# Attention and hash-routed experts on one core: loads four pairs ahead, casts three ahead, scatters queued behind the casts, the table filled in four pieces

## The chip, the cores and the metric

The kernel runs on one core of a Trainium2 chip. The metric is the device time of one execution in microseconds (us). Engines are named as in the profile: PE (TensorE) with its weight loads PEld, DVE (VectorE), ACT (ScalarE), POOL (GpSimd), SP (SyncE). A "q" behind a name is the engine's sequencer, which issues DMAs.

## The reference

Self-attention over 8 batches, 8 heads, 576 positions of 64 values in float32, with a relative position bias from a table of 32 buckets, is followed by a hash-routed mixture of 8 experts:

```
scores = q @ k^T / sqrt(64) + bias_table[bucket(|i - j|)]
x      = softmax(scores) @ v                 # 4608 tokens x 512
e      = token_id * 2654435761 % 8           # expert of a token
out    = relu(x @ w1[e]) @ w2[e]             # w1: 512 x 1024, w2: 1024 x 512
```

## The kernel before

**Attention** runs over 32 pairs of heads (4 pairs a batch). `load` (L165) brings q, k and v of a pair as float32 by eight DMAs on SP's queue, into tiles with four buffers (`qf`, `kf`, `vf`). `cast_qk` and `cast_v` (L187, L197) make float16 of them on POOL. `transposes` (L378) turns q and k on PE into PSUM (`pq`, `pk`, from the tag `aux` with two buffers, which `px` shares) and copies them on DVE to `qt` and `kz`. `scores` (L414) makes five score tiles in a two-buffer PSUM tile `ps`; ACT takes the exponential (L436, and L464 for the short fifth tile `atts`, of which there is one a pair), and DVE multiplies the band near the diagonal by `ebd` (L452, L469), the exponential of the bias. `av_steps` (L473) multiplies by v on PE into `px`, and DVE normalises into `x_all` (L501, L502). The scores of pair n are interleaved on PE with the products of pair n-1. All 45 product matmuls, 18 score matmuls and 12 transposes of a pair are placed by hand in PE's program; the order on the other engines is made by the scheduler of the framework.

In iteration n the program loads, casts and transposes pair n+2. After the last pair of a batch `dispatch` (L515) issues five indirect DMAs on POOL, which scatter the batch's tokens to the rows of their expert in the table `t_xperm`. The table is first filled with a padding row `zx` by one DMA of 5140 KB on ACT's queue (`fill_table`, L275). `route` (L281) computes each token's row from the token ids; it is called in iteration 1. The bias becomes `ebd` by two small matmuls (L234), an exponential (L239), one DMA to the DRAM tensor `t_f` (L243) and 16 DMAs back (L254), half on SP's queue and half on ACT's. The weights of the first two experts are loaded with a cast to float16 by POOL's queue (`load_w1`, `load_w2`; in program order at iteration 20 and behind the last, but the scheduler moved them to the start).

**A DMA's semaphore.** The framework gives the DMAs of SP and ACT together eight semaphores in turn (POOL's have eight of their own). A DMA waits at its issue until the one eight places earlier in that turn has landed.

**Experts**: per expert, a table block of 640 rows is loaded (`x_load`, L572), turned (L588), multiplied by w1 (L607), put through ReLU on ACT (L613), multiplied by w2 (L625), copied (L632) and scattered to the output (L633). This part is the same in both kernels but for the order of the first block loads.

Of the kernel before, what the change touches and what calls it, by code (L numbers as in the profile page):

```python
# [11 lines left out]
F32 = mybir.dt.float32  # L12
# [19 lines left out]
def kernel(  # L32
# [71 lines left out]
    F_d = nc.dram_tensor("t5_f", [H, D // 2, FW + 1], F16, kind="Internal")  # L104
# [41 lines left out]
    with tc.tile_pool(name="at", bufs=1) as at, tc.tile_pool(  # L146
# [40 lines left out]
        def cast_qk(n):  # L187
            for dst, src, name in ((qh, qf, "qh"), (kh, kf, "kh")):
                dst[n] = at.tile([PB, 2 * NBLK, 2, D], F16, name=name, bufs=3)
                nc.gpsimd.tensor_copy(  # L190
                    out=dst[n][:, :, :, :].transpose([0, 2, 1, 3]),
                    in_=src[n][:, :, :, :].rearrange(
                        "p h k (c d) -> p h (k c) d", c=2
                    ),
                )
# [8 lines left out]

        for n in range(2):
            load(n)

        tbl = at.tile([NB, H], F32, name="tbl")
        nc.sync.dma_start(out=tbl[:, :], in_=bias_table)
        ohsb = at.tile([NB, FW], F32, name="ohsb")  # L210
        nc.scalar.dma_start(out=ohsb[:, :], in_=OH_d.ap())
        nc.sync.dma_start(out=ident[:, :], in_=I128_d.ap())

        cast_qk(0)
        cast_qk(1)
        for i, z in enumerate(kz):
            nc.vector.memset(z[D:P, :, 0, :], 0.0)
            nc.vector.memset(z[:D, :, 1, :], 0.0)
        for i, x in enumerate(va):
            for hh in range(2):  # L220
                r0, r1 = D * hh, D * hh + D
                o0, o1 = D - D * hh, P - D * hh
                c0 = hh * (D + 1)
                nc.gpsimd.memset(x[o0:o1, :, c0 : c0 + D + 1], 0.0)
                nc.gpsimd.memset(x[r0:r1, :, c0 + D : c0 + D + 1], 1.0)
            if i < 2:
                cast_v(i)

        bps = atp.tile([P, 3, 512], F32, name="bps", tag="ps", bufs=2,
                       space=bass.MemoryType.PSUM)  # L230
        FH = (FW + 1) // 2
        for i in range(2):
            f0, f1 = FH * i, min(FH * i + FH, FW)
            nc.tensor.matmul(  # L234
                out=bps[:H, i, : f1 - f0], lhsT=tbl[:, :],
                rhs=ohsb[:, f0:f1],
            )
        ebsb = at.tile([H, 2, FH], F16, name="ebsb")
        nc.scalar.activation(  # L239
            out=ebsb[:, :, :], in_=bps[:H, :2, :FH], func=AF.Exp, bias=0.0,  # L240
            scale=1.0,
        )
        nc.sync.dma_start(  # L243
            out=F_d.ap()[:, :, :FW],
            in_=ebsb[:, :, :].rearrange("h a b -> h (a b)")[:, :FW]
            .unsqueeze(1).to_broadcast([H, HD, FW]),
        )
        for o in range(2):
            for c in range(2):
                for hh in range(2):  # L250
                    for cj in range(2):
                        eng = nc.sync if hh == 0 else nc.scalar
                        r0 = D * hh + HD * cj
                        eng.dma_start(  # L254
                            out=ebd[r0 : r0 + HD, :, c, o, :],
                            in_=bass.AP(
                                F_d.ap().tensor,
                                hh * HD * (FW + 1) + (o - cj + 1) * FY
                                + MAXD - 1 - D - HD * c,
                                [[FW, HD], [2 * HD * (FW + 1), NPAIR],  # L260
                                 [1, WB]],
                            ),
                        )
        nc.sync.dma_start(out=tok[:, :], in_=TOK_d.ap())
        nc.sync.dma_start(out=msk[:, :], in_=MSK_d.ap())
        nc.sync.dma_start(out=sltsb[:, :], in_=SLT_d.ap())
        tid32 = moe_token_ids.bitcast(I32)
        nc.sync.dma_start(
            out=er[:, :], in_=bass.AP(tid32.tensor, 0, [[2 * S, B], [1, 2 * S]])
        )  # L270
        zx = at.tile([P, XW], F16, name="zx")
        nc.gpsimd.memset(zx[:, :DM], 0.0)
        nc.gpsimd.memset(zx[:, DM:XW].bitcast(I32), BIG)

        def fill_table():  # L275
            nc.scalar.dma_start(
                out=xperm_d.ap()[:NSLOT, :].rearrange("(p r) d -> p r d", p=P),
                in_=zx[:, :].unsqueeze(1).to_broadcast([P, NSLOT // P, XW]),
            )
# [98 lines left out]
        def transposes(n):  # L378
            b, m = pairs[n]
            pq = aux([P, S], F16, "pq")  # L380
            pk = aux([P, S], F16, "pk")
            for k3 in range(NBLK):
                for c in range(2):
                    x = 2 * k3 + c
                    o = UA * c + PB * k3 if k3 < 2 else QW + UB * c
                    nc.tensor.transpose(  # L386
                        out=pq[:, o : o + PB],
                        in_=qh[n][:, x, :, :].rearrange("p h d -> p (h d)"),
                        identity=ident[:PB, :PB],
                    )  # L390
            for k3 in range(NBLK):
                for c in range(2):
                    x = 2 * k3 + c
                    o = HALF * c + PB * k3
                    nc.tensor.transpose(
                        out=pk[:, o : o + PB],
                        in_=kh[n][:, x, :, :].rearrange("p h d -> p (h d)"),
# [3 lines left out]
            nc.vector.tensor_copy(out=qt[:, :], in_=pq[:, :])  # L401
            z = kz[n % 3]
# [9 lines left out]
            qts[n], ktz[n] = qt, z  # L412

        def scores(n, g):  # L414
# [10 lines left out]
            if g < NDUO:  # L425
# [13 lines left out]
                )  # L439
                u0 = max(D * g - D, 0)  # L440
# [15 lines left out]
            else:  # L456
                kt = z[:, 2 * NDUO, :, :].rearrange("p h u -> p (h u)")
                for r in range(2):
                    nc.tensor.matmul(
                        out=ps[:, r, :HALF], lhsT=kt,  # L460
                        rhs=qt[:, HALF * r : HALF * r + HALF],
                        start=True, stop=True,
                    )
                nc.scalar.activation(  # L464
                    out=ats[:, :].rearrange("p (r i) -> p r i", r=2),
                    in_=ps[:, :2, :HALF], func=AF.Exp, bias=0.0, scale=scale,
                )
# [5 lines left out]
        def av_steps(n):  # L473
# [3 lines left out]
            for its in ((0, 1, 2), (3, 4)):  # L477
# [34 lines left out]
                )  # L512
                yield

        def dispatch(b):  # L515
            for t in range(NIT):
                sc_in = nc.gpsimd.indirect_dma_start(  # L517
                    out=xperm_d.ap()[:, :],
                    out_offset=bass.IndirectOffsetOnAxis(
                        ap=ds2[:, B * t + b : B * t + b + 1], axis=0  # L520
# [256 lines left out]
```

## Time and profile before

| | us |
|---|---|
| median of 3 runs (544.93 to 824.42) | 544.97 |
| the profiled execution's own time | 544.6 |
| its span, first to last instruction | 542.7 |
| PE busy | 364.1 (67%) |
| DVE, ACT, POOL busy | 216.0, 208.8, 197.5 |
| largest shares of the chain that ended last | PE 31%, issue 28%, DMA 20%, POOL 13% |

The span is what the prediction adds up; 1.9 us lie around it. Busy shares are means over stages with different limits, so the stages are read apart: the start (to 56 us), the first pairs, the steady pairs, the step to the experts, and the experts (from 384.4 us).

### The profile page before, as it was taken

The numbers are of one execution on the slowest core, as the hardware profiler recorded it, in microseconds if no ns is written. First come the engines' busy times: TensorE is split into PE (matmuls) and PEld (weight loads), VectorE is DVE, ScalarE is ACT, GpSimd is POOL, SyncE is SP. The second block draws the span as 40 slices with busy tenths as digits, with TensorE's granted clock in tenths as the row PEclk, the third lists the DMA queues.
The fourth block names the chain that finished last, engine by engine and source line by source line (L and its number), as shares of the span: only waits on it lengthen the run. The fifth ranks groups of instructions, "written<-read, shape, count | busy, mean of one in ns | idle before, by whom it ended". The sixth has DMA issues, their size and how long they took to land.

```text
span 542.7 us, 8776 instructions
## 1 busy us (share of the span) xinstructions
PE 364.1 (67%) x3403; PEld 267.1 (49%) x3403; DVE 216.0 (40%) x553; ACT 208.8 (38%) x226; POOL 197.5 (36%) x248
## 2 busy tenths in 40 slices
PE   0000736928938658469389387492799999999992
PEld 0000325727727547357277276471556655665561
DVE  1000337726727627456257276171132223223311
ACT  0000413726817627447358167180313421441240
POOL 9000224066074272390570751603042344234212
PEclk9999957968959959879879689697799999999997
DMA  8996968627147055172171330001469999999512
GB/s 189 186 232 151 163 154 210 152 83 184 42 125 182 21 144 144 40 197 72 61 203 43 111 89 12 34 1 53 138 157 161 222 240 194 197 230 233 124 46 81
DMA packets 109179, 71.90 MB, mean 132 GB/s; under 512 B 45983, under 2 KB 101535, under 8 KB 109128
## 3 DMA queue, kind: packets, MB, share of 16 engines
q0 software_dynamic: 17664, 30.96, 26.2%
q1 hardware_dynamic: 85128, 34.52, 24.6%
q10 hardware_dynamic: 6336, 5.76, 4.9%
q8 instruction: 29, 0.48, 0.4%
q14 instruction: 22, 0.18, 0.1%
HBM read 68.16 MB, written 21.41 MB: 165 GB/s over the span
## 4 chain that ended last, share of the span: by engine, by line
PE 31%; issue 28%; DMA 20%; POOL 13%; SPq 4%; DVE 1%; ACT 1%; POOLq 1%; ACTq 0%
PE hps L607 13%; PE ops L625 13%; DMA t_xperm<-zx 8%; DMA t_xperm<-x_all,ds 6%; POOL va L200 5%; POOL kh L190 4%; POOL t_xperm L517 3%; PE px L491 2%; DMA t_f<-ebsb 2%; PE xps L588 2%; SPq L180 2%; SPq L170 1%; DMA vf<-in_v_dram 1%; DMA kf<-in_k_dram 1%; PE ps L428 1%
## 5 line engine op out<-in xcount | busy, mean ns | idle before, releaser
L436 ACT ACTIVATE att<-ps 128x1152 f16<-128x1152 f32 x128 | 144.3, 1130 | 147.0 <-issue 80.8
L491 PE MATMUL px<-va,att 128*128 128x130 f16 x1280 | 114.2, 237 | 16.1 <-DVE att L452 8.1
L491 PEld LDWEIGHTS <-att 128*128 128x128 f16 x1280 | 98.1, 107 | 31.1 <-issue 14.6
L452 DVE TENSOR_TENSOR att<-att,ebd 128x512 f16<-128x512 f16 (+1 forms) x192 | 76.9, 430 | 58.2 <-ACT att L436 56.7
L613 ACT ACTIVATE h<-hps 128x640 f16<-128x640 f32 x64 | 45.0, 704 | 113.0 <-PE hps L607 113.0
L428 PE MATMUL ps<-qt,kz 128*128 128x384 f16 x256 | 83.8, 365 | 1.1 <-ACT att L436 1.1
L200 POOL CAST va<-vf 64x576 f16<-64x576 f32 x64 | 45.8, 716 | 103.2 <-DMA vf<-in_v_dram 56.8
L517 POOL DMA_INDIRECT t_xperm<-x_all,ds x40 | 39.3, 982 | 109.0 <-DVE x_all L502 80.6
L625 PE MATMUL ops<-w2t,h 128*128 128x512 f16 x320 | 72.7, 379 | 0.0
L607 PE MATMUL hps<-xpt,w1t 128*128 128x320 f16 x512 | 71.8, 301 | 0.1
L432 PE MATMUL ps<-qt,kz 128*128 128x192 f16 x256 | 68.6, 268 | 0.0
L607 PEld LDWEIGHTS <-w1t 128*128 128x128 f16 x512 | 50.3, 98 | 21.0 <-issue 0.3
L633 POOL DMA_INDIRECT out_dram<-ok,xpn x40 | 39.2, 979 | 57.4 <-DVE ok L632 51.3
L386 PE MATMUL pq<-ident,qh 96*128 96x96 f16 x192 | 15.9, 228 | 65.6 <-POOL qh L190 65.5
L386 PEld LDWEIGHTS <-qh 96*128 96x128 f16 x192 | 12.7, 108 | 70.5 <-POOL qh L190 67.9
L625 PEld LDWEIGHTS <-h 128*128 128x128 f16 x320 | 30.7, 98 | 33.5
L632 DVE COPY ok<-ops 128x512 f32<-128x512 f32 x40 | 27.7, 691 | 47.0 <-PE ops L625 47.0
L592 DVE COPY xpt<-xps 128x640 f16<-128x640 f16 x32 | 15.1, 489 | 73.9 <-PE xps L588 59.3
L401 DVE COPY qt<-pq 128x576 f16<-128x576 f16 x32 | 14.4, 451 | 67.3 <-PE pq L386 67.3
L234 PE MATMUL bps<-ohsb,tbl 32*8 32x384 f32 x4 | 2.7, 828 | 54.9 <-DMA tbl<-in_bias_table_dram 54.9
L491 PE MATMUL px<-va,atts 128*128 128x130 f16 x160 | 37.1, 232 | 0.3 <-ACT atts L464 0.3
L428 PEld LDWEIGHTS <-kz 128*128 128x128 f16 x256 | 27.6, 108 | 11.6 <-issue 4.7
(57 smaller groups left out, 310.2 us busy)
## 6 DMA issues: line engine op xcount, KB each, us to landing
qf<-in_q_dram SPq DMA_DIRECT2D x64, 144.0 KB, 2.7
kf<-in_k_dram SPq DMA_DIRECT2D x64, 144.0 KB, 3.1
vf<-in_v_dram SPq DMA_DIRECT2D x128, 72.0 KB, 2.7
w1t<-in_moe_w_dram POOLq DMA_DIRECT2D x8, 1024.0 KB, 9.9
w2t<-in_moe_w_dram POOLq DMA_DIRECT2D x8, 1024.0 KB, 10.5
t_xperm<-zx ACTq DMA_DIRECT2D x1, 5140.0 KB
xpn<-t_xperm SPq DMA_DIRECT2D x8, 642.5 KB, 8.5
t_xperm<-x_all,ds POOLq DMA_INDIRECT x40, 2.5
```

The costliest lines, as they stand in the source:

```text
L200: nc.gpsimd.tensor_copy(out=va[n % 4][r0:r1, :, hh * (D + 1) : hh * (D + 1) + D], in_=vf[n][r0:r1, :, :],)
L386: nc.tensor.transpose(out=pq[:, o : o + PB], in_=qh[n][:, x, :, :].rearrange("p h d -> p (h d)"), identity=ident[:PB, :PB],)
L428: nc.tensor.matmul(out=ps[:, c, :QW], lhsT=kt, rhs=qt[:, :QW], start=True, stop=True,)
L432: nc.tensor.matmul(out=ps[:, 2, RW * c : RW * c + RW], lhsT=kt, rhs=qt[:, QW:], start=True, stop=True,)
L436: nc.scalar.activation(out=att[:, g, :, :], in_=ps[:, :, :QW], func=AF.Exp, bias=0.0, scale=scale,)
L452: nc.vector.tensor_tensor(out=a, in0=a, in1=ebd[:, m, :, :, a0 + w0 : a1 + w0], op=ALU.mult,)
L491: nc.tensor.matmul(out=px[:, ii, :, :].rearrange("p h d -> p (h d)"), lhsT=lhsT, rhs=vb[:, t, :], start=(x == 0), stop=(x == len(todo) - 1 ...
L517: sc_in = nc.gpsimd.indirect_dma_start(out=xperm_d.ap()[:, :], out_offset=bass.IndirectOffsetOnAxis(ap=ds2[:, B * t + b : B * t + b + 1], ...
L607: nc.tensor.matmul(out=hps[:, nr, :NR], lhsT=w1h[:, kt, ts(ft, P)], rhs=xt[e][:, kt, ts(nr, NR)], start=(kt == 0), stop=(kt == NPT - 1),)
L613: nc.scalar.activation(out=h1[:, ft, :].rearrange("p (r n) -> p r n", r=NRC), in_=hps[:, :, :NR], func=AF.Relu, bias=0.0, scale=1.0,)
L625: nc.tensor.matmul(out=ops[:, :], lhsT=h1[:, ft, ts(kc, P)], rhs=w2h[:, ft, :], start=(ft == 0), stop=(ft == NFT - 1),)
L633: so = nc.gpsimd.indirect_dma_start(out=out[:, :], out_offset=bass.IndirectOffsetOnAxis(ap=xn[e][:, kc, DM:XW].bitcast(I32), axis=0), in_= ...
```

## The change

The names stay; what moves is the order, by hand on all five engines. In iteration n the kernel now loads pair n+4, casts v of pair n+2 and q and k of pair n+3, transposes q of pair n+2 ahead of the fifth score tile and k behind it, and multiplies the band of a score tile one tile later than its scores. A batch's five scatters are put on a list once a batch is past, and at most two are issued an iteration, behind the casts, from iteration 8; those of the last batch follow right on their rows. The fill of the table is four DMAs of a quarter each on SP's queue in iterations 2 to 5. Four weight loads stand in iterations 20, 22, 25 and 28. `route` is called in iteration 0. The tensor `t_f` has skewed rows, so that `ebd` is read by 4 DMAs on 128 partitions instead of 16 on 32; it is written by two DMAs on ACT's queue. All small loads of the start are on ACT's queue. The k cast of pair 0 is on DVE.

```diff
-            if i < 2:
-                cast_v(i)
...
-        def fill_table():
-            nc.scalar.dma_start(
-                out=xperm_d.ap()[:NSLOT, :].rearrange("(p r) d -> p r d", p=P),
-                in_=zx[:, :].unsqueeze(1).to_broadcast([P, NSLOT // P, XW]),
-            )
...
+        def band(n, g):
+            m = pairs[n][1]
+            att, ats = atts[n]
...
+        load(0)
+        tbl = at.tile([NB, H], F32, name="tbl")
+        nc.scalar.dma_start(out=tbl[:, :], in_=bias_table)
...
+        va_init(0)
+        cast_qk(0, nc.vector)
+        load(1)
...
+        for cj in range(2):
+            nc.scalar.dma_start(
+                out=bass.AP(
+                    F_d.ap().tensor, cj * HD * PW,
+                    [[D * PW, H], [PW + 1, HD], [1, 2 * FY]],
+                ),
...
+        transpose_q(0)
+        transpose_k(0)
+        cast_v(0)
+        cast_qk(1)
+        for o in range(2):
+            for c in range(2):
+                nc.sync.dma_start(
+                    out=ebd[:, :, c, o, :],
...
+        load(2)
+        load(3)
+        va_init(1)
+        cast_v(1)
+        cast_qk(2)
...
+        FILLS = 4
+
+        def fill_table(i):
+            rows = NSLOT // FILLS
+            nc.sync.dma_start(
...
-            transposes(0)
-            transposes(1)
-            for n in range(NP + 1):
-                av = av_steps(n - 1) if n > 0 else iter(())
-                if n < NP:
-                    if n + 2 < NP:
-                        load(n + 2)
-                        cast_qk(n + 2)
-                        cast_v(n + 2)
-                    for g in range(NIT):
-                        scores(n, g)
-                        if g < NDUO:
-                            advance(av, 12)
-                    advance(av, 99)
-                    if n + 2 < NP:
-                        transposes(n + 2)
-                    if n == 1:
-                        fill_table()
-                        route()
...
-                if n > 0 and pairs[n - 1][1] == NPAIR - 1:
-                    dispatch(pairs[n - 1][0])
+            if n + 4 < NP:
+                load(n + 4)
+            if 2 <= n < 2 + FILLS:
+                fill_table(n - 2)
+            if n + 2 < NP:
+                cast_v(n + 2)
+            if n + 3 < NP:
+                cast_qk(n + 3)
+            if n >= 5 and pairs[n - 1][1] == 0:
+                waiting += [(pairs[n - 5][0], t) for t in range(NIT)]
+            if n >= 8:
+                for _ in range(2):
+                    if waiting:
+                        dispatch(*waiting.pop(0))
...
+            for g in range(NIT):
+                scores(n, g)
+                if g < NDUO:
+                    advance(av, 12)
+                else:
+                    advance(av, 99)
+                if g == 0 and n > 0:
+                    band(n - 1, NIT - 1)
+                elif g > 0:
+                    band(n, g - 1)
+                if g == NDUO - 1:
+                    advance(av, 99)
+                    if n == 0:
+                        transpose_q(1)
+                        transpose_k(1)
+                        route()
+                    if n + 2 < NP:
+                        transpose_q(n + 2)
+            if n + 2 < NP:
+                transpose_k(n + 2)
```

**POOL, at the end of a batch, before.** `va` is the float16 v of a pair, `qh` and `kh` its q and k, and the rows with `t_xperm` are scatters.

```order
L190 CAST kh<-kf 96x2x6x64
L200 CAST va_79<-vf 64x9x64
L517 DMA t_xperm<-x_all,ds_59 9728x514 x4
L200 CAST va_79<-vf 64x9x64
L517 DMA t_xperm<-x_all,ds_59 9728x514
L190 CAST qh<-qf 96x2x6x64
```

POOL in the change, from the first iterations that have scatters:

```order
L203 CAST va_81<-vf 64x9x64 x2
L193 CAST qh<-qf 96x2x6x64
L193 CAST kh<-kf 96x2x6x64
L455 DMA t_xperm<-x_all,ds_59 9728x514 x2
L203 CAST va_78<-vf 64x9x64 x2
```

Four scatters stood between the two halves of a v cast, with the q and k casts of the same pair behind them; now two stand behind the casts of a pair.

**ACT, from the first instruction, before**; its DMAs are on ACT's queue:

```order
L211 DMA ohsb<-t_bias_oh 32x768
L276 DMA t_xperm<-zx 5120x1x514
L239 ACT_TABLE_LOAD
L239 ACTIVATE ebsb<-bps 8x768
L436 ACTIVATE att<-ps 128x1152 x4
```

SP in the change, from the last loads of pair 6 to the second quarter (the loads of a pair are `qf`, `kf` and `vf`):

```order
L181 DMA vf<-in_v_dram 32x9x64 x4
L558 DMA t_xperm<-zx 1280x1x514
L171 DMA qf<-in_q_dram 96x3x128 x2
L171 DMA kf<-in_k_dram 96x3x128 x2
L181 DMA vf<-in_v_dram 32x9x64 x4
L558 DMA t_xperm<-zx 1280x1x514
```

The whole fill was ACT's second DMA; its first quarter now stands on SP behind the loads of pair 6, and the others behind one more pair's loads each.

**DVE, one pair, before** (from the band of the fifth tile of pair n-1, L469, to the band of pair n's fourth tile):

```order
L469 TENSOR_TENSOR atts<-atts,ebd 128x192
L401 COPY qt<-pq 128x576
L404 COPY kz_77<-pk 64x9x64 x2
L452 TENSOR_TENSOR att<-att,ebd 128x4x128
L452 TENSOR_TENSOR att<-att,ebd 128x768
L501 RECIPROCAL rcp<-px 128x6
L502 TENSOR_TENSOR x_all<-px,rcp 128x3x128
L452 TENSOR_TENSOR att<-att,ebd 128x4x128
L452 TENSOR_TENSOR att<-att,ebd 128x4x64
L501 RECIPROCAL rcp<-px 128x4
L502 TENSOR_TENSOR x_all<-px,rcp 128x2x128
L452 TENSOR_TENSOR att<-att,ebd 128x4x64
```

DVE in the change, over the same stretch:

```order
L406 TENSOR_TENSOR atts<-atts,ebd 128x192
L400 TENSOR_TENSOR att<-att,ebd 128x4x128
L438 RECIPROCAL rcp<-px 128x6
L439 TENSOR_TENSOR x_all<-px,rcp 128x3x128
L400 TENSOR_TENSOR att<-att,ebd 128x768
L438 RECIPROCAL rcp<-px 128x4
L439 TENSOR_TENSOR x_all<-px,rcp 128x2x128
L400 TENSOR_TENSOR att<-att,ebd 128x4x128
L400 TENSOR_TENSOR att<-att,ebd 128x4x64
L318 COPY qt<-pq 128x576
L400 TENSOR_TENSOR att<-att,ebd 128x4x64
L400 TENSOR_TENSOR att<-att,ebd 128x384
```

The instructions are the same; the normalising (`rcp`, `x_all`) moved ahead of a band product, and the copies of q and k are no longer together.

## Rows read from the trace of the kernel before

**Rows 1.** Windows by stage; busy us (count) by engine, granted clock, DMA share, GB/s.
```profile
0.00:56.00 56.00, 1.14 (x2) 0.24 (x3) 2.22 (x9) 1.28 (x1) 15.43 (x36) 1.00 0.93 185
56.00:98.60 42.60, 26.68 (x208) 18.86 (x206) 22.65 (x62) 15.04 (x16) 11.67 (x15) 0.72 0.81 184
98.60:366.40 267.80, 183.85 (x2163) 154.41 (x2163) 146.07 (x404) 146.75 (x146) 115.96 (x141) 0.83 0.35 95
366.40:384.40 18.00, 3.96 (x52) 3.39 (x51) 2.91 (x10) 0.69 (x2) 4.87 (x5) 0.68 0.39 128
384.40:542.70 158.30, 148.49 (x982) 90.21 (x981) 42.14 (x71) 45.04 (x64) 49.60 (x52) 0.97 0.74 163
```

**Rows 2.** Timeline of the start: start us, duration us, engine, line, operation, tiles.
```profile
0.74 0.91 SPq L170 DMA_DIRECT2D qf<-in_q_dram  x2
2.77 1.97 SPq L180 DMA_DIRECT2D vf<-in_v_dram  x4
6.80 45.85 SPq L180 DMA_DIRECT2D vf<-in_v_dram  x4
8.53 0.58 ACTq L276 DMA_DIRECT2D t_xperm<-zx  x1
74.45 0.26 DVE L469 TENSOR_TENSOR atts<-atts,ebd 128x192 f16<-128x192 f16 x1 [5.79 <-DMA ebd<-t_f]
```

**Rows 3.** Waits of SP's queue: line, what it waited for, us in total, times, longest.
```profile
SPq L180 <- DMA t_xperm<-zx: 44.1, 1, 44.1
```

**Rows 4.** Chain that ended last, in order of time: start us, us, what.
```profile
8.53 42.79 DMA t_xperm<-zx
59.42 10.26 DMA t_f<-ebsb
378.43 5.40 DMA xpn<-t_xperm
```

**Rows 5.** Waits of the engines, same columns as Rows 3.
```profile
POOL t_xperm L517 <- DVE x_all L502: 80.6, 7, 11.5
PE pq L386 <- POOL qh L190: 65.5, 8, 9.5
```

**Rows 6.** Timeline at a batch's end; the bracket has the engine's idle time before.
```profile
186.04 0.98 POOL L517 DMA_INDIRECT t_xperm<-x_all,ds  x1 [11.51 <-DVE x_all L502]
192.71 0.68 POOL L200 CAST va<-vf 64x576 f16<-64x576 f32 x1 [1.85 <-DMA t_xperm<-x_all,ds]
194.69 0.82 POOL L190 CAST qh<-qf 96x768 f16<-96x768 f32 x1
195.57 0.66 PE L386 MATMUL pq<-ident,qh 96*128 96x96 f16 x6 [9.25 <-POOL qh L190]
```

**Rows 7.** Windows of three pairs, each from one fifth-tile exponential to the next.
```profile
174.34:180.48 6.14, 5.66 (x75) 4.82 (x75) 4.68 (x15) 5.06 (x7) 0.19 (x1) 1.00 0.04 12
186.62:204.62 18.00, 8.91 (x81) 7.31 (x81) 5.33 (x15) 5.07 (x7) 13.40 (x17) 0.62 0.49 137
204.62:211.79 7.17, 5.66 (x75) 4.82 (x75) 5.71 (x15) 5.05 (x6) 2.99 (x5) 1.00 0.87 216
```

**Rows 8.** Timeline inside the first and the last pair of Rows 7.
```profile
175.70 1.13 ACT L436 ACTIVATE att<-ps 128x1152 f16<-128x1152 f32 x1 [0.72 <-ACT atts L464]
180.85 0.41 PE L395 MATMUL pk<-ident,kh 96*128 96x96 f16 x6 [0.41 <-DVE x_all L502]
207.00 0.63 PE L491 MATMUL px<-va,att 128*128 128x130 f16 x8 [1.19 <-DVE qt L401]
```

**Rows 9.** DMA issues: tiles, queue, count, KB each, median us from issue to landing.
```profile
vf<-in_v_dram SPq DMA_DIRECT2D x128, 72.0 KB, 2.7
w1t<-in_moe_w_dram POOLq DMA_DIRECT2D x8, 1024.0 KB, 9.9
```

**Rows 10.** Timeline of ACT: fifth-tile exponentials of pairs 1 and 2.
```profile
84.55 0.65 ACT L464 ACTIVATE atts<-ps 128x576 f16<-128x576 f32 x1
98.58 0.65 ACT L464 ACTIVATE atts<-ps 128x576 f16<-128x576 f32 x1
```

More of the change, by code (lines that the diff above doesn't have):

```diff
@@ L203, in cast_v @@
                 )
[L205 to L218, printed above, removed]
@@ L248 @@
[L248 to L263, printed above, removed]
@@ L439, in scores @@
                 )
+            else:
+                kt = z[:, 2 * NDUO, :, :].rearrange("p h u -> p (h u)")
+                for r in range(2):
+                    nc.tensor.matmul(
+                        out=ps[:, r, :HALF], lhsT=kt,
+                        rhs=qt[:, HALF * r : HALF * r + HALF],
+                        start=True, stop=True,
+                    )
+                nc.scalar.activation(
+                    out=ats[:, :].rearrange("p (r i) -> p r i", r=2),
+                    in_=ps[:, :2, :HALF], func=AF.Exp, bias=0.0, scale=scale,
+                )
+        def band(n, g):
+            m = pairs[n][1]
+            att, ats = atts[n]
+            if g < NDUO:
                 u0 = max(D * g - D, 0)
@@ L512, in av_steps, with dispatch @@
                 )
+                if done is not None:
+                    done(its)
                 yield
[L515 to L520, printed above, removed]
-                    ),
-                    in_=x_all[:, b, t, :],
-                    in_offset=None,
-                    bounds_check=NROW - 1,
-                    oob_is_err=False,
-                )
-                disjoint(sc_in, "xrows")
+        def dispatch(b, t):
+            sc_in = nc.gpsimd.indirect_dma_start(
+                out=xperm_d.ap()[:, :],
+                out_offset=bass.IndirectOffsetOnAxis(
+                    ap=ds2[:, B * t + b : B * t + b + 1], axis=0
+                ),
+                in_=x_all[:, b, t, :],
+                in_offset=None,
+                bounds_check=NROW - 1,
+                oob_is_err=False,
+            )
+            disjoint(sc_in, "xrows")
         def advance(it, count):
@@ new lines @@
+        guard = tc.manual_schedule(engines={
+            E_ALL.PE, E_ALL.Activation, E_ALL.Pool, E_ALL.SP, E_ALL.DVE,
+        })
+        guard.__enter__()
+        load(0)
+        tbl = at.tile([NB, H], F32, name="tbl")
+        nc.scalar.dma_start(out=tbl[:, :], in_=bias_table)
+        ohsb = at.tile([NB, FW], F32, name="ohsb")
+        nc.scalar.dma_start(out=ohsb[:, :], in_=OH_d.ap())
+        nc.scalar.dma_start(out=ident[:, :], in_=I128_d.ap())
+        tid32 = moe_token_ids.bitcast(I32)
@@ new lines @@
+        va_init(0)
+        cast_qk(0, nc.vector)
+        load(1)
+        bps = atp.tile([P, 3, 512], F32, name="bps", tag="ps", bufs=2,
+                       space=bass.MemoryType.PSUM)
+        FH = FW // 2
+        for i in range(2):
+            nc.tensor.matmul(
+                out=bps[:H, i, :FH], lhsT=tbl[:, :],
+                rhs=ohsb[:, FH * i : FH * i + FH],
+            )
+        ebsb = at.tile([H, 2, FH], F16, name="ebsb")
+        nc.scalar.activation(
+            out=ebsb[:, :, :], in_=bps[:H, :2, :FH], func=AF.Exp, bias=0.0,
+            scale=1.0,
+        )
@@ L565 @@
+            if n + 2 < NP:
+                transpose_k(n + 2)
+            if n == NP - 1:
+                band(n, NIT - 1)
+        assert not waiting
+        guard.__exit__(None, None, None)
     with tc.tile_pool(name="mo", bufs=1) as mo, tc.tile_pool(
```

161 lines of the change are left out of this document (86 added, 75 removed).

## The prediction

> **What bounds the kernel now.** I read the windows by stage first, since the page's shares average over stages with different limits [rows 1]. The experts take 158.3 us with PE busy for 148.5 of them: they are bound by PE, and the change leaves their order alone. The 267.8 us of steady pairs have PE busy for 184 and no other engine over 147: nothing is full there, so something waits. In the first 56 us PE works for 1.1 us.
>
> The timeline, SP's waits and the chain tell why the start is empty. SP stands 45.85 us on the last loads of pair 1 [rows 2]; it waits 44.1 us for the fill of the table [rows 3], which takes 42.79 us in the chain [rows 4]. The load needs the semaphore that the fill still holds, and the bias table and the loads of pair 2 queue behind it.
>
> The waits of the engines show the second hole: POOL's scatters wait 80.6 us for `x_all`, 7 times, and PE's q transposes wait 65.5 us for POOL's casts [rows 5]. At a batch's end [rows 6] POOL has stood 11.51 us, because a scatter of rows not yet made is ahead of the casts in its program. Then come four scatters, 1.85 us for their landing and a fifth scatter before the q cast at 194.69, and PE resumes at 195.57 after 9.25 us idle. A pair there takes 18.0 us at a granted clock of 0.62, an undisturbed one 6.14 at 1.00 [rows 7].
>
> The third reading is the pair whose casts lie beside its DVE work: 7.17 us, DVE busy 5.71 instead of 4.68, POOL 2.99 instead of 0.19, and the clock still at 1.00, its 2.4 GHz level [rows 7].
>
> **The change part by part.** I add up a new span in four terms: the time of pair 0's fifth-tile exponential, 31 intervals to pair 31's, the step to the experts, the experts.
>
> *Start.* Nothing waits for the fill any more. SP issues a pair's eight loads in 4.0 us, 0.74 to 4.74 [rows 2], and each takes 2.7 us to land [rows 9]. Two pairs' loads, the second held up a little by the landing of the first, are in at about 13. The first write of `t_f` waits for the last of them, eight places back. That write took 10.26 us beside other loads [rows 4]. It now moves 512 KB instead of 384 with nothing beside it, so I bound it by 4 us (an issue and a landing as of a load) and 13.7 (the same rate), and keep 10.3, the row of this very transfer. Reading `ebd` back took from 69.7, the end of that write, to DVE's start at 74.45 [rows 2, 4], 4.8 us; four DMAs instead of 16 carry the same bytes. So DVE starts the first band at about 28. Behind it in DVE's program are three band products and the copies of pair 1, some 3 of a pair's 4.7 us of DVE [rows 7], and then `route`. The interval that held `route` was 14.03 us [rows 10] against 6.14: 7.9 us. Pair 0's fifth exponential then starts at about **40**; bounds 30 (the quick write, half of `route` beside PE's work) and 46 (the slow write, and landings late).
>
> *Steady pairs.* The 7 batch ends cost 18.0 - 6.14 = 11.9 us each, 83 in all, and go if the casts run ahead. POOL has 3.0 us of casts a pair and at most two scatters behind them; four scatters filled 186.04 to 190.86 [rows 6], so 1.2 each, 2.4 for two. That is 5.4 us, or 6.4 with the issue of a weight load as long as a scatter's. A v cast waits for PE to free its buffer, so POOL starts a pair's casts when PE ends the products of the pair before, and ends q and k 3.0 later; PE wants them about a pair after that. The 2.5 us landing that a v cast waited for at a batch's end (rows 6 show the 1.85 of it that were left) lies within that.
>
> But now every pair has casts beside its DVE work, and 7.17 is the row nearest to it; 6.14 is a pair without them. DVE's extra 1.03 us went straight into the pair: in both it idles 1.46. The new order can return some of the idle time. PE waited 0.41 for `x_all` before k's transposes and ACT 0.72 at the change of pairs; with casts beside, PE waited 1.19 for the copy of q [rows 8]. In the change the fifth score tile stands between the two transposes, and the bands trail by a tile. The copy of q still stands behind a band product, and the next products need its PSUM slot. I take back 0.4 of 7.17: **6.8 a pair**, 31 of them 210.8. The floor is DVE's 5.71; ACT's 5.06 and PE's 5.66 are below it. With POOL feeding it, PE keeps the busy share of the 7.17 pair, at whose clock of 1.00 I leave it.
>
> Here a rule speaks against the change. Rows 7 show that 2.99 us of casts cost DVE 1.03, about a third. The Trainium skill (SBUF — State Buffer, Who interferes with whom) says that a VectorE instruction with two SBUF inputs and a GpSimd one that reads SBUF exclude each other, whichever starts first blocking the other wholly. The band products and the casts are such a couple. By the rule a pair may pay all its casts; it is rival B.
>
> *DMA.* SP's issue needs 4.0 us a pair of 6.8. A quarter of the fill costs between (42.79 - 3 x 9.9) / 4 = 3.3, if the three weight loads that ran beside it are taken off [rows 4, 9], and 42.79 / 4 = 10.7. Loads and a quarter so take 7.3 to 14.7 us, late by 0.5 to 7.9 four times: 2 to 32. A pair's loads are let go when the v cast four pairs earlier is done, three pairs or 20 us before they are needed. That leaves 0 to 12 us; I take 0, since the fill moved beside those weights. In iterations 20 to 27 three weight loads of 9.9 and eight pairs' loads of 4.0 make 62 us in 54: 8 late, inside the 20. Cover gone, these 8 would show.
>
> *Step to the experts.* 18.0 us [rows 1]. The last batch's five scatters stay in the way; the first of three blocks, which together took 5.40 [rows 4], is now ahead of the others. I take 1 off: 17, between 16 and 18. *Experts:* 158.3.
>
> **Sum.** 40 + 210.8 + 17 + 158.3 = 426.1 us of span, and 1.9 around it as before (544.6 - 542.7): **428**. The profiled execution is 0.4 below the median of 544.97, which I leave out. As a balance: pair 1's exponential comes at 46.8 instead of 84.55, 30 intervals of 9.4 become 6.8, 1 at the step: 38 + 78 + 1 = 117 less.
>
> **Rivals.**
> A, the forecast: pairs of 6.4 to 7.3, 416 to 444.
> B, the casts are paid in full: 6.14 + 2.99 = 9.1 a pair, 40 + 283 + 175.3 + 1.9 = 500. For it: a band product and a cast do slow each other. Against it: the contended pair has paid a third.
> C, the loads come late under the fill, by the upper bound 12 us: 440. SP's program puts a quarter between two pairs' loads, and a load eight places behind a quarter cannot be issued before the quarter has landed; so loads four ahead may be so in the program only. Against it: the lead of three pairs.
> D, the order hides the contention: 6.0 a pair, a little above DVE's 5.71: 403. For it: 1.46 us of DVE's idle time in rows 7 come from the old order. Against it: DVE waits for ACT and PE in the new order too.
> E, slower. POOL loses its lead and each pair waits for its own casts as a batch's end did. That pair's 18.0, less the 7.9 that scatters and their landing take from 186.04 to 194.65 without the one cast in between, is 10.1; with two scatters 12.5, with one 11.3. The change has 15 pairs with two, 5 with one and 11 with none in 31: 355 us, a total of 572. It decides from a mean of (544.6 - 1.9 - 175.3 - 40) / 31 = 10.6 us a pair. For it: POOL is busy 5.4 to 6.4 of 6.8, so it has little to catch up with, and PE at 1.2 GHz would stretch what it waits for. Against it: PE asks for the casts a whole pair later than they are made.
>
> **How the numbers follow.** A 0.67, C 0.12, D 0.10, B 0.07, E 0.04. The time is A's. The range of 402 to 455 holds A with its start between 30 and 46, C (also with slower pairs) and most of D; it leaves out B and E and some 0.07 of the edges. Two per cent, about 11 us and about what a measurement of this kernel can tell from no change, lies far from all but E: faster 0.95, within 2% 0.01, slower 0.04.
>
> **What would show it.** SP's long wait for the fill is gone, and PE starts transposes before 15 us. DVE's first band product comes at 28 and waits for `ebd`. From pair 1 on the intervals between fifth-tile exponentials are even, 6.4 to 7.3, at clock 1.00, with DVE the fullest engine and band products lengthened by casts. Q's transposes no longer wait for POOL. The forecast is wrong if intervals in iterations 2 to 8 or 20 to 28 are much longer than the rest (C), if most exceed 8 (B), if they alternate with the number of scatters (E), or if the start is not near 40.

## The result, and the profile after

The changed kernel takes **430.69 us** (median; 428.3 to 432.97) against 545.34 for the kernel before on the same chip: a ratio of 0.790 [0.785, 0.795]. 428 was forecast. The profiled execution took 428.3 us, its span is 426.5. Ratios leave out the one slow execution each of the kernel before (824.42), x_all (728.7) and x_lead (446.81); the medians contain it, and without it they are 544.97, 411.38 and 440.56.

Windows by stage after the change (columns as in [rows 1]): pairs 1 to 4, pairs 14 and 15, pairs 22 to 24, the step, the experts.

```profile
47.80:73.20 25.40, 22.63 (x300) 18.82 (x300) 24.16 (x57) 20.25 (x21) 12.29 (x17) 1.00 1.13 207
131.00:148.20 17.20, 11.69 (x152) 9.53 (x153) 11.18 (x32) 10.34 (x10) 10.39 (x14) 0.98 0.48 135
187.00:212.60 25.60, 18.80 (x225) 15.32 (x225) 16.44 (x46) 15.52 (x17) 12.83 (x16) 0.93 0.95 199
250.30:268.20 17.90, 4.17 (x56) 3.87 (x57) 3.60 (x12) 0.64 (x2) 4.86 (x5) 0.68 0.42 134
268.20:426.50 158.30, 148.41 (x980) 89.95 (x978) 41.78 (x71) 45.04 (x64) 49.60 (x52) 0.97 0.74 163
```

The early pairs take 6.35 us each, with DVE busy 95% of it. In the second window two pairs take 17.2 and DVE is busy for 11.2: there something waits, as in the third.

Timeline after: the write of `t_f`, its reading back, DVE's first band, the fifth tile's exponentials of pairs 0 and 31.

```profile
8.28 1.94 ACTq L522 DMA_DIRECT2D t_f<-ebsb  x2
20.09 2.05 SPq L536 DMA_DIRECT2D ebd<-t_f  x4
25.41 1.43 DVE L400 TENSOR_TENSOR att<-att,ebd 128x512 f16<-128x512 f16 x4 [15.96 <-DMA ebd<-t_f]
38.95 0.65 ACT L379 ACTIVATE atts<-ps 128x576 f16<-128x576 f32 x1 [23.77 <-PE ps L374]
250.30 0.65 ACT L379 ACTIVATE atts<-ps 128x576 f16<-128x576 f32 x1
```

From 38.95 to 250.30 there are 31 intervals, 6.82 us in the mean. They are not even. Read from the starts of those exponentials and numbered by the pair they begin with (the expectations of x_onecast and x_weights count from 1), intervals 1 to 6 are 6.35 to 6.40; 14 and 15 are 7.63 and 9.61; 22 to 25 are 7.80, 8.02, 9.78 and 7.12. Interval 0, in which `route` ends, is 8.87.

Waits of the engines and of SP's queue after (columns as in [rows 3]).

```profile
POOL va L203 <- issue: 21.8, 9, 5.4
PE pq L310 <- POOL qh L193: 12.1, 6, 3.9
```
```profile
SPq L181 <- POOL va L203: 31.8, 13, 5.3
SPq L181 <- DMA t_xperm<-zx: 5.9, 4, 1.8
```

The wait for the fill has gone from 44.1 to 5.9 us [rows 3], that of the q transposes from 65.5 to 12.1 [rows 5]. New is POOL's v cast, which waits for nothing that the profile can name; SP's loads of v wait for that cast. POOL's timeline around pairs 15 and 22 shows when it starts.

```profile
140.22 0.97 POOL L455 DMA_INDIRECT t_xperm<-x_all,ds  x1 [0.32 <-DVE kz L335]
141.18 0.78 POOL L203 CAST va<-vf 64x576 f16<-64x576 f32 x1
145.67 0.68 POOL L203 CAST va<-vf 64x576 f16<-64x576 f32 x1 [3.71 <-issue]
...
184.83 1.03 POOL L455 DMA_INDIRECT t_xperm<-x_all,ds  x1 [0.30 <-issue]
185.85 0.96 POOL L203 CAST va<-vf 64x576 f16<-64x576 f32 x1
192.25 0.68 POOL L203 CAST va<-vf 64x576 f16<-64x576 f32 x1 [5.45 <-DMA vf<-in_v_dram]
```

The scatter issued at 140.22 landed at 145.47, that of 184.83 at 192.06, behind a weight load that POOL had issued at 179.31 and that landed at 188.52. Each time the second half of v is cast 0.2 us after the landing. In the trace this cast carries a wait for the semaphores of the two scatters ahead of it, though it shares no data with them; the first half carries none. The same wait was there before, once a batch (the 1.85 us in [rows 6]); now it stands in every pair with a scatter.

### The profile page after: what moved, and what is told of

It is laid out like the page before. It is cut to its first block, busy times and chain, and to the rows that moved or that the text cites. A ratio compares the mean times of both kernels' runs of the same rounds, so it can differ in the third digit from the quotient of the medians.

```text
span 426.5 us, 8764 instructions
## 1 busy us (share of the span) xinstructions
PE 345.1 (81%) x3403; PEld 250.2 (59%) x3403; DVE 233.0 (55%) x554; ACT 209.8 (49%) x226; POOL 200.6 (47%) x247
## 5 line engine op out<-in xcount | busy, mean ns | idle before, releaser
L428 PE MATMUL px<-va,att 128*128 128x130 f16 x1280 | 104.1, 225 | 9.2 <-DVE qt L318 8.6
L400 DVE TENSOR_TENSOR att<-att,ebd 128x512 f16<-128x512 f16 (+1 forms) x192 | 95.2, 524 | 19.4 <-DMA ebd<-t_f 16.0
L428 PEld LDWEIGHTS <-att 128*128 128x128 f16 x1280 | 89.6, 100 | 21.4 <-issue 12.3
L359 PE MATMUL ps<-qt,kz 128*128 128x384 f16 x256 | 77.5, 342 | 1.7 <-DVE kz L335 1.0
L363 PE MATMUL ps<-qt,kz 128*128 128x192 f16 x256 | 65.2, 255 | 0.0
L379 ACT ACTIVATE atts<-ps 128x576 f16<-128x576 f32 x32 | 20.8, 650 | 36.6 <-PE ps L374 32.7
L193 POOL CAST qh<-qf 96x768 f16<-96x768 f32 x32 | 27.8, 869 | 17.5 <-DMA qf<-in_q_dram 14.7
L428 PE MATMUL px<-va,atts 128*128 128x130 f16 x160 | 35.4, 221 | 0.0
L439 DVE TENSOR_TENSOR x_all<-px,rcp 128x384 f16<-128x384 f32 x64 | 31.4, 491 | 2.2
L128 POOL DMA_DIRECT2D w1t<-in_moe_w_dram x8 | 6.5, 808 | 51.8 <-PE xps L649 51.8
## 6 DMA issues: line engine op xcount, KB each, us to landing
w2t<-in_moe_w_dram POOLq DMA_DIRECT2D x8, 1024.0 KB, 10.1
xpn<-t_xperm SPq DMA_DIRECT2D x8, 642.5 KB, 12.1
```

The lines of the kernel that those rows point to most:

```text
L359: nc.tensor.matmul(out=ps[:, c, :QW], lhsT=kt, rhs=qt[:, :QW], start=True, stop=True,)
L363: nc.tensor.matmul(out=ps[:, 2, RW * c : RW * c + RW], lhsT=kt, rhs=qt[:, QW:], start=True, stop=True,)
L400: nc.vector.tensor_tensor(out=a, in0=a, in1=ebd[:, m, :, :, a0 + w0 : a1 + w0], op=ALU.mult,)
L428: nc.tensor.matmul(out=px[:, ii, :, :].rearrange("p h d -> p (h d)"), lhsT=lhsT, rhs=vb[:, t, :], start=(x == 0), stop=(x == len(todo) - 1 ...
L439: nc.vector.tensor_tensor(out=x_all[:, b, its[0] : its[0] + ni, P * m : P * m + P].rearrange("p t (h d) -> p t h d", h=2), in0=px[:, :, :, ...
```

## The experiments

Times stand against 430.69 of the changed kernel; ratios are to the kernel before, run beside each.

### What makes the slow stretches

**x_onecast.** The two loads of v write the diagonal blocks of a zeroed buffer, and one cast takes both halves.

```diff
-            for hh in range(2):
-                nc.gpsimd.tensor_copy(out=va[n % 4][r0:r1, ...], in_=vf[n][r0:r1, :, :])
+            nc.gpsimd.tensor_copy(out=va...[:, :, :, :D], in_=vf[n][:, :, :, :])
```

> Both halves of v in one cast per pair (128 partitions x 9 x 128, the zeros of the off-diagonal halves kept in four fixed load buffers), so that no cast of POOL has a wait for the two scatters just issued; same work otherwise. Theory (the slow stretches around pairs 14 to 16 and 23 to 26 come from POOL's second v cast, which waits for the scatters to land): intervals between the fifth tiles' exps stay at 6.36 throughout, 31 x 6.36 = 197 against 211 now, so about 417 us, ratio 0.967 to the changed kernel; SP's wait for POOL's v cast (31.8 us in 13) falls below 10. Rival (loads themselves are late beside scatters and weight loads): the stretches stay, 428 to 432. Second rival (one cast of 1152 columns takes longer than two of 576): POOL above 3.3 us a pair and no gain.

433.7 us, ratio 0.794 [0.791, 0.798]. The waits for scatters are gone from the program and the stretches with them: intervals 10 to 27 all lie between 6.98 and 6.99, beside scatters and weight loads alike. That could be the slack of a slower pair; but x_slots below, with the same scatters and weight loads and the single cast of v at 5.9 to 6.4 a pair, has no interval from 10 to 28 over 6.43 either. So their cause is shown. But the expected gain was taken back elsewhere, by neither rival: POOL works less (95 us on casts against 101.7), and yet nearly every interval is 6.98 in place of 6.36. SP's wait for the cast of v, forecast under 10 us, is 17.5. Windows of x_onecast, four early pairs and the old second stretch:

```profile
49.40:77.40 28.00, 22.62 (x300) 18.82 (x300) 23.98 (x57) 20.36 (x22) 11.81 (x13) 1.00 1.15 202
131.00:148.00 17.00, 13.91 (x184) 11.32 (x182) 14.67 (x34) 12.49 (x14) 11.01 (x11) 1.00 0.71 180
```

**x_weights.**

```diff
-            if n == 20: load_w1(0)   # and 22, 25, 28
+            if n == 4: load_w1(0)    # and 5, 6, 7
```

> The four weight loads on POOL's queue are issued at pairs 4 to 7, ahead of the first scatter, in place of pairs 20, 22, 25, 28. Theory (a scatter that is issued behind a weight load on POOL's queue lands after 7.1 us in place of 3.6, and the cast behind it waits): intervals 23 to 26, now 7.80, 8.02, 9.78, 7.12, fall to 6.4 to 7, 5 us less; the weights now run beside the pieces of the table fill, which may cost 0 to 8 us in pairs 4 to 9: 425 to 433 us. Rival (the stretch at pairs 23 to 26 has nothing to do with the weights): it stays.

448.59 us, ratio 0.822 [0.817, 0.826]: worse than either expectation. Intervals 22 to 25 are now 5.88, 6.60, 7.80 and 5.67, so the late stretch did shrink; but a load of q behind weights and fill came 12.5 us late, interval 7 took 19.75, and seven of the next eight, with scatters that landed after up to 7.8, took 7.6 to 9.8. In pairs 1 to 4 the DMA share is 1.13 already without the weights (first window above).

### What a cast costs

**x_tinycast**:

```diff
-                cast_qk(n + 3)
+                (cast_qk if n + 3 < 12 else cast_tiny)(n + 3)   # cast_v likewise
```

> From pair 12 on POOL casts one column per tile in place of whole q, k and v (stale data from the earlier pairs is computed on), with the same instructions, waits, loads and scatters. Theory (POOL's casts lengthen DVE's bands, 524 ns against 430 in the kernel before, and DVE at 6.1 of 6.36 us is what bounds an undisturbed pair): bands from pair 12 on at about 430, DVE 5.3 a pair, intervals 5.7 to 5.9 (PE's 5.66 is next), no stretch around pair 14, about 20 x 0.55 + 12 = 23 us less: 408. Rival (casts cost DVE nothing, the bands are longer for another reason): bands stay at 520, intervals 6.36, and only the slow stretches go: 418.

406.79 us, ratio 0.745 [0.741, 0.749]. This kernel leaves out nearly all of the casting from pair 12 on and computes on stale data; it measures what the casts cost. It came as the theory had it: 5.88 in 16 of the 19 intervals 10 to 28, no stretch at pair 14, and bands of 383 ns in the mean from pair 12 on (423 over the whole trace). A window of some 11 pairs shows which engine is left full: PE, 60.78 of 64 us.

```profile
148.00:212.00 64.00, 60.78 (x825) 51.59 (x822) 50.18 (x153) 54.86 (x55) 24.54 (x58) 1.00 0.96 204
```

To see what a cast does to a band, POOL's and DVE's timelines of one pair of x_onecast are laid side by side.

```profile
55.94 1.15 POOL L202 CAST va<-vfz 128x1152 f16<-128x1152 f32 x1 [4.04 <-PE px L429]
57.04 1.02 POOL L194 CAST qh<-qf 96x768 f16<-96x768 f32 x1
58.00 0.88 POOL L194 CAST kh<-kf 96x768 f16<-96x768 f32 x1
...
56.13 0.42 DVE L440 TENSOR_TENSOR x_all<-px,rcp 128x256 f16<-128x256 f32 x1
56.47 1.72 DVE L401 TENSOR_TENSOR att<-att,ebd 128x512 f16<-128x512 f16 x2
58.12 0.45 DVE L319 COPY qt<-pq 128x576 f16<-128x576 f16 x1
58.48 0.81 DVE L401 TENSOR_TENSOR att<-att,ebd 128x256 f16<-128x256 f16 x2
```

The two bands at 56.47 meet the casts of v and q and end 0.3 and 0.14 us after them; in a free pair the same two take 0.61 (below). The copy `qt`, which reads PSUM, lies wholly under the cast of k and takes its 0.45. Counted over the whole trace of x_onecast, 73 of 192 bands begin under a cast (at least 0.05 us after its start and 0.1 before its end). **None of them ends before the cast**, the earliest 0.14 us after it. The 46 of 128 x 256 among them take 717 ns in the mean, the 15 of this size that meet no cast 282. The 25 copies `qt` that begin under a cast take 446, the six that meet none 448. The changed kernel gives the same: 54 such bands, none done before the cast. Beside a scatter's issue alone bands are not longer: those of 128 x 512 take 422 there (10) and 418 free (19).

It works the other way round too. In the changed kernel 14 casts begin, on an idle POOL, while a band runs that no earlier cast holds up; each of these bands takes its usual time, and the cast ends 0.5 to 0.9 us after it. POOL's and DVE's timelines there show both ways within 1 us:

```profile
176.78 0.68 POOL L203 CAST va<-vf 64x576 f16<-64x576 f32 x1 [1.82 <-issue]
177.53 1.05 POOL L193 CAST qh<-qf 96x768 f16<-96x768 f32 x1
...
176.82 0.74 DVE L406 TENSOR_TENSOR atts<-atts,ebd 128x192 f16<-128x192 f16 x1
177.49 0.41 DVE L400 TENSOR_TENSOR att<-att,ebd 128x512 f16<-128x512 f16 x1
```

The cast of v starts first, and a band that takes 0.26 when free takes 0.74; then the band starts first and takes its 0.41, and the cast of q takes 1.05 instead of 0.82.

That is the rule of the Trainium skill that the prediction weighed (SBUF — State Buffer, Who interferes with whom): of a VectorE instruction with two SBUF inputs and a GpSimd one that reads SBUF, whoever starts first blocks the other; one with at most one SBUF input, outside VectorE's fast two-port modes, does not contend. The rows agree but for two kinds. Two bands of the changed kernel that began less than 0.02 us after a cast's start ended first. And a cast directly behind a scatter can win against a band that began earlier: in x_slots it did so in all 10 cases, by 0.21 to 0.27 us, in the changed kernel in one of 13; why, no run here shows. Once, in x_onecast, such a band stood behind all three casts of a pair (interval 9, 8.87; two bands in the row):

```profile
102.97 3.57 DVE L401 TENSOR_TENSOR att<-att,ebd 128x512 f16<-128x512 f16 x2
```

Then a cast's price is what DVE happens to do beside it, and should be movable.

**x_slots** moves the casts (one of v, as above) to where DVE reads PSUM or waits.

```diff
+  after_band(cast_v(n + 2), band(n, 0))              # at tile 1
+  after_band(cast_qk(n + 3, only="k"), band(n, 1))   # at tile 2, scatters behind it
+  after_band(cast_qk(n + 3, only="q"), band(n, 3))   # at tile 4, before transpose_k
```

> One cast of v per pair as in x_onecast, and each of POOL's three casts now starts behind a named band of DVE: v behind the next pair's first band (DVE's next 1.6 us are a wait and two reads of PSUM), k behind the second tile's band, q behind the fourth tile's bands (two reads of PSUM of 0.45 us follow); scatters and weight loads between k and q. The casts and their number are the same. Theory (a band that meets a running cast ends only once the cast has ended, a read of PSUM beside a cast is not lengthened, so the price of a cast is set by what DVE does beside it): bands near 430 ns in place of 524 and 572, intervals 5.9 to 6.1, 402 to 409 us, against 430.7 and 433.7. Rival (a cast costs DVE the same wherever it stands): intervals 6.36 to 7, 418 to 434. Second rival (the waits make POOL late and the transposes wait for qh): single intervals over 7 beside scatters.

417.79 us, ratio 0.763 [0.759, 0.768]. Pairs 1 to 6 take 5.88 each with all their casts. One of them, POOL's and DVE's timelines:

```profile
60.47 0.82 POOL L205 CAST kh<-kf 96x768 f16<-96x768 f32 x1 [0.92 <-DVE att L413]
62.77 0.82 POOL L205 CAST qh<-qf 96x768 f16<-96x768 f32 x1 [1.47 <-DVE att L413]
...
115.71 0.97 POOL L469 DMA_INDIRECT t_xperm<-x_all,ds  x1 [0.30 <-DMA qf<-in_q_dram]
116.68 0.84 POOL L205 CAST qh<-qf 96x768 f16<-96x768 f32 x1
...
61.25 0.61 DVE L413 TENSOR_TENSOR att<-att,ebd 128x512 f16<-128x512 f16 x2
61.78 0.45 DVE L331 COPY qt<-pq 128x576 f16<-128x576 f16 x1
62.62 0.92 DVE L348 COPY kz<-pk 64x576 f16<-64x576 f16 x2
63.57 0.26 DVE L420 TENSOR_TENSOR atts<-atts,ebd 128x192 f16<-128x192 f16 x1
...
116.45 1.19 DVE L420 TENSOR_TENSOR atts<-atts,ebd 128x192 f16<-128x192 f16 x1
```

The cast at 62.77 lies under the two copies `kz`; the band after it takes 0.26. At 115.71 a second scatter makes the cast of q late, it meets that band, and 0.26 becomes 1.19 (the band began 0.23 us ahead of the cast's record: one of the 10 cases above). Pairs with two scatters take 6.3 to 6.4. So the first theory holds and the rival (the same price anywhere) falls. The expected 402 to 409 was missed because of this, of a late load at pair 7 (intervals 7 to 9 are 8.77, 7.00 and 7.09), of interval 29 (8.18) and of a start that came 1.7 us later.

### What the parts of the change are worth

**x_bandnow**, each band right behind its scores:

```diff
                 scores(n, g)
+                band(n, g)
```

> Each tile's band multiply stands right after its scores again, as in the kernel before, instead of one tile later; everything else as changed. Theory (the order is worth 0.4 to 0.8 us a pair, since a band one tile late never holds DVE up for its exp): undisturbed intervals 6.8 to 7.2 in place of 6.36, 444 to 456 us. Rival (the pair's time is DVE's sum and the order of its work gives nothing): 6.36 stays, 428 to 433 us.

461.12 us, ratio 0.843 [0.840, 0.847]. Undisturbed intervals 7.1 to 7.6, every few one of 9.2: 30 us more, above either expectation. Two of its waits, the first of which (bands waiting for their exponential) was 3.5 in the changed kernel:

```profile
DVE att L400 <- ACT att L367: 68.7, 89, 2.2
...
PE pq L310 <- DVE x_all L439: 31.4, 28, 2.1
```

**x_onefill**, one transfer on ACT's queue:

```diff
-        FILLS = 4
+        FILLS = 1      # and nc.scalar in place of nc.sync
```

> The table fill is one transfer of 5.1 MB on ACT's queue at pair 2, as it was in the kernel before, in place of four pieces on SP's queue at pairs 2 to 5. Theory (a load of SP that shares the fill's semaphore waits for all of it, and the loads ahead cover 4 pairs of 6.4 us against 26 us or more of filling): one or two intervals between pairs 4 and 8 of 12 to 25 us, 440 to 455. Rival (the loads four pairs ahead cover it whatever its form): 429 to 435.

448.94 us, ratio 0.821 [0.815, 0.826]. SP's loads wait 38.0 us for the fill once, the v cast of a pair waits 24 us for its load, and one interval takes 21.81.

```profile
SPq L181 <- DMA t_xperm<-zx: 38.0, 1, 38.0
```
```profile
78.57 0.68 POOL L203 CAST va<-vf 64x576 f16<-64x576 f32 x1 [23.97 <-DMA vf<-in_v_dram]
```

**x_lead**:

```diff
-            if n + 3 < NP:
-                cast_qk(n + 3)
+            if 1 <= n and n + 2 < NP:
+                cast_qk(n + 2)
```

> q and k are cast two pairs ahead in place of three, everything else as changed. Theory (the third pair of lead is what keeps PE's transposes from waiting for POOL, and a scatter that lands late now shows at once): PE's transposes wait for POOL's qh some 2 us in most pairs and 3 to 6 beside scatters, as in the kernel before (65.5 us in 8); intervals 6.4 to 8, 445 to 475. Rival (POOL is early enough either way): 429 to 435.

442.6 us, ratio 0.810 [0.803, 0.817]. Intervals 1 to 5, without scatters, keep 6.36; 7 to 14 take 7.5 to 9.2. The q transposes wait 24.2 us in 14 pairs, twice the changed kernel's: the mechanism of the theory, at a little less than its size.

### The start, and a faster kernel

**x_wide**:

```diff
-                out=bps[:H, i, :FH], lhsT=tbl[:, :],
+                out=bps[:, i, :FH], lhsT=tblx...,   # each head's column 16 times
...
-                [[D * PW, H], [PW + 1, HD], [1, 2 * FY]]
+                [[D * PW, H], [2 * (PW + 1), 16], [PW + 1, 2], [1, 2 * FY]]
```

> The table of biases is computed on all 128 partitions (each head 16 times, by a weight matrix with repeated columns), and the two writes of t_f read it from 128 partitions with two copies each, not from 8 partitions with 32 copies; the same 512 KB go to the same rows. Theory (the write is slow because its source lies on 8 partitions): t_f lands 3 to 5 us after its issue in place of 11.8, the first band starts at 18 to 20 in place of 25.4, the fifth tile's exp of pair 0 at 32 to 34 in place of 38.95, all 5 to 7 us less: 424 to 426. Rival (the rows written bound it, or the loads beside it): no change, 429 to 433.

434.18 us, ratio 0.793 [0.788, 0.799]: no gain, but not for the rival's reason. The write is issued at 10.95 and has landed at 16.98, by its semaphores: 6.0 us, against 11.8 (8.28 to 20.07) in the changed kernel, so the 3 to 5 of the theory were not quite reached. Its issue comes 2.7 later, since the repeated columns are made behind another cast on DVE; the first band is at 22.2 and the exponential of pair 0 at 35.4. What this won was lost in longer intervals (up to 10.1): POOL's v cast waits 34.6 us in place of 21.8 without a releaser in the profile, and interval 29 takes 8.89 in place of 6.19. Windows of the changed kernel and of x_wide during the write:

```profile
12.00:14.00 2.00, 2.00 (x11) 1.20 (x10) 0.00 (x0) 1.82 (x2) 0.00 (x0) 1.00 0.47 64
```
```profile
14.00:16.00 2.00, 1.74 (x9) 0.87 (x8) 0.00 (x0) 1.82 (x3) 1.67 (x4) 1.00 0.54 177
```

At about the same DMA share, 64 GB/s become 177: each busy engine moves more, not more engines. The Trainium skill (DMA: Bandwidth & Descriptors, Why a DMA increments its semaphore by 16 and not by 1) says that a transfer runs on the largest number of engines, up to 16, that divides the slowest dimension (of a size over 1) of both its sides; by that it would be 8 in both kernels, since `t_f` is written by 8 heads. The trace agrees: the semaphore of each write rises in eight steps as it lands, in either kernel (that of a load of `qf` in sixteen), and the shares are 0.47 and 0.54. Why a source on 8 partitions is slower for each engine no run here shows.

**x_spread** is x_slots with

```diff
-        FILLS = 4      # at pairs 2 to 5
+        FILLS = 8      # at pairs 1 to 8
...
-                for _ in range(2):
+                for _ in range(35 * (n - 9) // 22 - 35 * (n - 10) // 22):
```

> x_slots with the table fill in eight pieces at pairs 1 to 8 in place of four at 2 to 5, and the 35 scatters spread over pairs 10 to 31, one or two a pair, in place of two from pair 8 on. In x_slots the pairs without scatters take 5.88, pair 7 takes 8.77 (a load of k comes 7.3 late: 7.5 MB asked for in 4 pairs, some 205 GB/s moved), pairs with two scatters 6.3 to 6.4, because two of 1.3 us overrun the 2.1 us between the casts of k and q. Theory: pair 7 falls to 6 to 7 (-2 to -3), nine pairs with one scatter take 5.9 (-3 to -4 in all), 410 to 413 us against 417.8. Rival (transfers are at their limit however they are cut): the late load only moves, 416 to 420.

410.54 us, ratio 0.753 [0.750, 0.757]. Intervals 1 to 9 are 5.88, the late load of pair 7 is gone; pairs with one scatter take 5.9 to 6.1, with two 6.2 to 6.5.

**x_all** adds the wide write of `t_f`.

> x_spread with the write of t_f from 128 partitions, as in x_wide. Theory: in x_wide the fifth tile's exp of pair 0 came at 35.4 in place of 38.95, and what that gained was lost in scatter waits of the casts, which are gone here: 3 to 4 us below x_spread, 406 to 410. Rival (the loads are what the start waits for later, so a start 3.5 us earlier only waits longer for them): no difference to x_spread.

411.52 us, ratio 0.753 [0.750, 0.757]: the rival's time, but pair 0's exponential is at 39.0, so the start was not earlier at all. **x_best** changes where DVE zeroes the load buffers:

```diff
-        for z in vfz: ...            # four buffers ahead of everything
+        vfz_init(0)                  # the other three behind transpose_k(0)
```

> x_all with only the first of the four load buffers for v zeroed at the head of DVE's queue and the other three after pair 0's copies. In x_all the weight matrix with repeated columns stood behind eight memsets of DVE, the exp of the biases began at 13.3 (x_wide: 10.1), the first band at 25.9 (x_wide: 22.2), and the fifth tile's exp of pair 0 at 39.0 (x_wide: 35.4), so the earlier landing of t_f was spent there. Theory (that is why x_all came out like x_spread): first band at 22 to 23, the exp at 35 to 36, and as no cast waits for a scatter any more the 3 to 4 us stay: 406 to 409 us against 410.5. Rival (the loads of the next pairs bound the start): 410 to 412.

**404.95 us**, ratio 0.741 [0.738, 0.744]: the fastest, 26 us below the changed kernel. The exponential is at 36.1, 3.0 earlier than in x_spread, and this stays; most of the rest of the 5.6 us is interval 29, 6.31 in place of 8.81, which this edit does not explain. Ten early pairs take 58.8 us, PE busy 96%, DVE 78%:

```profile
45.70:104.50 58.80, 56.38 (x750) 46.93 (x750) 46.08 (x141) 50.67 (x52) 28.96 (x31) 1.00 1.10 212
```

**x_lastw** moves a single weight load:

```diff
-            if n == 28:
-                load_w2(1)
...
                 advance(av, 99)
+                load_w2(1)
```

> x_best with the last weight load of the attention part (w2 of the second expert) issued after the last pair in place of at pair 28. In x_slots, x_spread and x_all pair 29 or 30 takes 8.2 to 8.8 us where its neighbours take 5.4 to 6.3; PE pauses there with no releaser in the profile, some 4 to 8 us after that load's issue. Theory (the pause comes from that load, by whatever way): the interval falls to 5.5 to 6.4, 2 to 3 us less than x_best. Rival (the pause is unrelated to it, as the changed kernel and x_tinycast with the same load show none): the interval stays over 8.

409.38 us, ratio 0.749 [0.747, 0.752]. Nothing is decided: x_best itself, with the load at pair 28, has no long interval there, so that of 8.2 to 8.8 us in x_slots, x_spread and x_all remains unexplained, as does interval 29 of x_wide (8.89), x_onefill (8.40) and x_lead (7.98). The step to the experts grew: the weight load now runs beside the read of the experts' rows, for which PE waits 17.7 us in place of 12.8.

## Why the prediction was right, step by step

- **Start, 40.** Measured 38.95, by errors that cancel. The first of the two DMAs that write `t_f` was issued at 8.28, not 13: it waited for no load of pair 1 (the second, at 9.93, waited for the first load of that pair, not for the last). The write took 11.8, not the 10.3 that was kept: of its two bounds "the same rate" was the nearer, and its narrow source the reason (x_wide). Reading back took 5.3 against 4.8, and the first band came at 25.4 against 28. The four bands and the copies of pair 1 took 2.7 us, 3 by the forecast for three of them and the copies, and `route` to the exponential 10.8, from 28.16, against 7.9.
- **Steady pairs, 6.8.** The mean is 6.82, and that this fits is luck: two errors of 14 us cancel. An undisturbed pair is 6.36: the new order gives back 0.8 of [rows 7]'s 7.17, not 0.4 (with the old order in the same pipeline, x_bandnow, it is 7.1 to 7.6). The other 31 x (6.82 - 6.36) = 14 us are, within 1 us, what intervals 12 to 17 and 21 to 25 have over 6.36 (6.0 and 7.6); the 2.5 us of interval 0 and pairs below 6.36 nearly cancel. Here two steps failed. "The 2.5 us landing ... lies within that": in iterations 8 to 27 scatters landed after 3.0 to 5.3 us, and after 7.1 to 7.2 behind a weight load, and POOL, with casts of 3 and scatters of 2.4, has little room left in 6.36. "In iterations 20 to 27 ... 8 late, inside the 20": the weight loads' lateness did not come through the loads four pairs ahead but through the scatters in the same queue, which that lead does not cover.
- **"The floor is DVE's 5.71".** It was no floor. 1.03 of it was time in which bands stood behind casts; with the casts moved DVE needs 4.6 of 5.88 and PE, at 5.64, is the bound.
- **Rival B** had the rule right and its sum wrong: not every cast meets a band. At 6.36 the casts cost 0.48 a pair, in x_onecast 1.1, in x_slots, where no scatter is near, nothing.
- **DMA, 0.** Right for the changed kernel: no interval from 1 to 8 is over 6.40. In four pieces on SP's queue, in place of one on ACT's, the fill is worth 18 us (x_onefill). The cover is thin: at 5.88 a pair the same four pieces made pair 7 late.
- **Step, 17.** 17.9. The 1 us for the first block did not come, as the 5.40 of [rows 4] were misread: they are the second of three loads, not the three together. In the kernel before, too, the first block was the first to be loaded; it landed after 4.3 us (377.98 to 382.27), as it does now (261.40 to 265.72).
- **Experts, 158.3**, as measured.
- **Rivals.** The sign named for C, long intervals in iterations 20 to 28, did appear, but by late scatters and not by late loads; and the intervals were not even, as A's sign wanted. D came half (its 6.0 needs the casts moved too). E's mechanism was there without its size: POOL lost its lead in two places and had it back within four pairs.

## What to carry to other kernels

When two engines exclude each other over SBUF, do not count their overlap as a percentage: lay their timelines side by side and tie the off-path engine's work to a point where the busy one reads PSUM or waits. In a queue that works ahead, look at every wait that its instructions carry, also for data they do not touch: one that is harmless once a batch becomes a bound when the pipeline puts it into every turn. A sum that comes out right is no proof of its terms; the intervals, one by one, were.

## What the runs showed of the hardware

- A band that began at least 0.05 us after a cast's start on POOL and 0.1 before its end never ended before it, in any of the 159 cases of the changed kernel, x_onecast and x_best. Copies out of PSUM are not lengthened (446 against 448 ns), nor are bands beside a scatter's issue alone (422 against 418 for 128 x 512).
- One cast of 128 x 1152 elements takes 1.16 us in the mean (x_slots), two of 64 x 576 take 1.47 (the changed kernel).
- 512 KB written from 8 partitions landed after 11.8 us (the changed kernel), from 128 partitions after 6.0 (x_wide).
- In iterations 8 to 27 of the changed kernel a scatter landed after 3.0 to 5.3 us, and after 7.1 to 7.2 behind a 1 MB load on the same queue.
